# Moving the SBUF slots of a three-stage kernel's matmul operands to multiples of 512 bytes

## The chip, the cores and the metric

The kernel runs on one NeuronCore of a Trainium2 chip. The metric is the device time of one execution in microseconds (us). TensorE is PE in the profile, its weight loads are PEld, VectorE is DVE, ScalarE is ACT, GpSimd is POOL and SyncE, which issues nearly all transfers, is SP.

## The reference

Four sequences of 3072 tokens with 256 features pass through three stages.

```python
scores = (1.0 / S) * np.matmul(z, z.transpose(0, 2, 1))     # z: 4 x 3072 x 64
out = u * np.matmul(np.maximum(scores, 0.0) ** 2, v)        # u, v: 4 x 3072 x 256
h = out @ w_in                                              # 256 -> 2048
x = (h - np.tanh(h)) @ w_out                                # 2048 -> 256
xk = mu_k * x + (1.0 - mu_k) * x_prev                       # x_prev: the token before, 0 at a sequence's start
xr = mu_r * x + (1.0 - mu_r) * x_prev
k = np.maximum(xk @ w_k, 0.0)                               # 256 -> 1024
result = 1.0 / (1.0 + np.exp(-(xr @ w_r))) * (k * k @ w_v)  # 1024 -> 256
```

`u`, `v`, `z` and the mixing vectors are float32. The weights are float64, and the kernel makes float32 of their high and low words during the attention.

## The kernel before

The work is cut into 24 blocks of 512 tokens (six a sequence). Features, or keys, lie on the 128 partitions and tokens along a partition, so every matmul has a moving operand of 128x512 and a stationary one of 128x128, both float32 read in one pass. To keep precision each operand is split into a high and a low part, and a product takes three matmuls (`PASSES`: high by high, high by low, low by high); the scores put both parts of the 64 features of z on the 128 partitions and take two.

A unit is `produce`, which writes a two-bank PSUM tile `w` and makes from it a high part `h` and a low part `l` of 128x1024 (on ACT and DVE), and `consume`, 12 matmuls that add the unit's product into `acc`. Units are A (attention, two chunks of 128 keys, 4 matmuls at L323 and L324), H (the 256 to 2048 to 256 feed-forward, 12 matmuls at L334), K (the channel mix, 12 matmuls at L334) and R (the gate, 12 matmuls at L358, and no consume). The loop issues `produce` of unit n and then `consume` of unit n-2 (`LAG`), all of it at L390. There are 288 A units, then for each of the 24 blocks 8 H, 4 K and 1 R; the K and R of a block are woven into the H of the next. That is 288x16 + 24x300 = 11808 matmuls, and 4584 of them stand before the first H matmul (288 produces of 4, 286 consumes of 12). PE's order is written out by this loop. All other work hangs on steps with a first and a last unit, which `run_steps` hands out after each unit by their costs; the engines run their queues in order.

Memory is a row of slots in each partition, in the order in which the pools first ask for them, each rounded up to 32 bytes. `mu` and `omu` (16 bytes each) come first, and everything else stands behind them. A slot's start, as the remainder by 512:

| tiles | what they are for matmuls | remainder before |
|---|---|---|
| `v`, `w_in`, `w_out`, `w_k`, `w_v` (tag big) | stationary | 32 |
| `h`, `l` of all units (tags hi, lo) | moving, at L390 | 32 |
| `xh`, `x`, `mkh`, `mkl`, `mrh`, `mrl` (tag p4) | moving, at L334 and L358 | 192 |
| `z1`, `z2` (tag p2, 11 slots) | both, at L323 and L324 | 192, 224, 256, ... 480, 0: 32 more from slot to slot |
| `w_r` (tag p2) | stationary, at L358 | 320 (high), 384 (low) |

The p2 slots walk because the tag also holds `x2`, which has 4 columns more than 512: 2064 bytes. Within a tile every operand begins at a multiple of 512 bytes from the tile's start, so these remainders are those of the operands.

`x2_steps` copies a block's H result from PSUM to `x2` (L412) behind a column 3 that holds the token ahead of the block: DVE copies it from the block before (L414) or writes 0 (L416). `mix_steps` then makes the mixed tokens: ACT scales the shifted columns 3 to 514 by `omu` (L430), DVE adds `mu` times the unshifted ones (L433), and two more steps split the sum into high and low.

Of the kernel before, what the change touches and what calls it, by code (L numbers as in the profile page):

```python
# [7 lines left out]
F32 = mybir.dt.float32  # L8
# [3 lines left out]
ACTF = mybir.ActivationFunctionType  # L12
ALU = mybir.AluOpType

P = 128
TB = 512
# [3 lines left out]
def relu2_attention__tanh_ffn__channel_mix_kernel(  # L20
# [20 lines left out]
    nc = tc.nc  # L41
# [4 lines left out]
    DC = D // P  # L46
    NG = S // TB
# [4 lines left out]
    scale = 1.0 / S  # L52
# [5 lines left out]
    sb = ctx.enter_context(tc.tile_pool(name="sb", bufs=1))  # L58
# [6 lines left out]
    def p4(name, dt=F32, shape=(P, 2, 512)):  # L65
        return sb.tile(list(shape), dt, tag="p4", name=name, bufs=10)

    def p2(name, dt=F32, n=512):
        return sb.tile([P, n], dt, tag="p2", name=name, bufs=NG + 5)

    mu = sb.tile([P, 2, DC], F32, name="mu")
    omu = sb.tile([P, 2, DC], F32, name="omu")
    x1d = [dr.tile([P, DC, TB], F32, name=f"x1d{t}") for t in range(NT)]

    def copy_hi(o, i):
# [2 lines left out]
    def sub_lo(o, i, hi):  # L78
        nc.vector.tensor_tensor(out=o, in0=i, in1=hi.bitcast(F32), op=ALU.subtract)  # L79
# [4 lines left out]
    def z_load(b, g):  # L84

        t = sb.tile([P, 16, 32], F32, tag="zs", name=f"zin{b}_{g}", bufs=3)
        src = z[b, g * TB : (g + 1) * TB, :].rearrange("(k j) (a i) -> a j k i", j=32, i=32)
        for h in range(P // DQ):
            for a in range(DQ // 32):
                q = nc.scalar if h and b == 0 and g == 0 else nc.sync  # L90
                q.dma_start(out=t[h * DQ + 32 * a : h * DQ + 32 * a + 32], in_=src[a])  # L91
        zin[b, g] = t

    def z_steps(b, g):
        st = {}

        def high():
            a = zin.pop((b, g))
            st["t"] = t = sb.tile([P, TB], F32, tag="zt", name=f"zt{b}_{g}", bufs=1)
            st["w"] = w = p2(f"z1_{b}_{g}", F32R)  # L100
            nc.vector.transpose(out=t, in_=a.rearrange("p k i -> p (k i)"))
            nc.vector.tensor_copy(w, t)

        def low():
            t, w = st["t"], st["w"]
            sub_lo(w[DQ:], t[DQ:], w[DQ:])
            if b == 0 and g == 0:
                z2[0] = w2 = p2("z2_0", F32R)
                sub_lo(w2[:DQ], t[:DQ], w[:DQ])
                copy_hi(w2[DQ:], t[DQ:])  # L110
            z1[b, g] = w

        return [(1.0, high), (0.7, low)]
# [8 lines left out]
    def v_load(b, g):  # L122
        t = p4(f"vr{b}_{g}", shape=(P, 4, D))
        nc.sync.dma_start(
            out=t, in_=v[b, g * TB : (g + 1) * TB, :].rearrange("(c p) d -> p c d", p=P)
        )
        vraw[b, g] = t

    def v_steps(b, g):
        st = {}  # L130

        def high():
            st["w"] = w = big(f"v{b}_{g}").rearrange("p (l c d) -> p l c d", l=2, c=4)
            copy_hi(w[:, 0], vraw[b, g])

        def low():
            w = st["w"]
            sub_lo(w[:, 1], vraw.pop((b, g)), w[:, 0])
            vs[b, g] = w

        return [(0.0, high), (1.3, low)]
# [127 lines left out]
    xraw, xs, x2t, mixed = {}, {}, {}, {}  # L269
# [105 lines left out]
    def consume(unit):  # L375
        kind, t, p = unit
        if kind == "R":
            return
        s = split.pop(unit)
        o = get_acc(kind, t)  # L380
        last = {"A": NP, "H": NH, "K": NK}[kind] - 1
        for j in range(2):
            f = 2 * p + j
            if kind == "A":
                w = [vs[t // NG, f // 4][:, l, f % 4] for l in range(2)]
            else:
                w = [x[:, f % 4] for x in ws["out" if kind == "H" else "v", f // 4]]
            for c in range(DC):
                for n, (a, m) in enumerate(PASSES):
                    nc.tensor.matmul(  # L390
                        o[:, c],
                        w[a][:, c * P : (c + 1) * P],
                        s[m][:, j],
                        start=p == 0 and j == 0 and n == 0,
                        stop=p == last and j == 1 and n == 2,
                    )
# [9 lines left out]
    def x2_steps(i):  # L406
        def f():
            o = acc.pop(("H", i))
            x2t[i] = []
            for c in range(DC):  # L410
                x = p2(f"x2_{i}_{c}", n=TB + 4)
                nc.scalar.activation(out=x[:, 4:], in_=o[:, c], func=ACTF.Copy)  # L412
                if i % NG:
                    nc.vector.tensor_copy(x[:, 3:4], x2t[i - 1][c][:, TB + 3 :])  # L414
                else:
                    nc.vector.memset(x[:, 3:4], 0.0)  # L416
                x2t[i].append(x)

        return [(0.2, f)]

    def mix_steps(which, i):
        m = 0 if which == "k" else 1
        st = {}

        def one(c):
            x = x2t[i][c]
            if c == 0:
                st["t"] = p4(f"mx{which}{i}")
            t = st["t"]
            nc.scalar.activation(  # L430
                out=t[:, c], in_=x[:, 3 : TB + 3], func=ACTF.Copy, scale=omu[:, m, c : c + 1]
            )
            nc.vector.scalar_tensor_tensor(  # L433
                out=t[:, c], in0=x[:, 4:], scalar=mu[:, m, c : c + 1], in1=t[:, c],
                op0=ALU.mult, op1=ALU.add,
            )

        def high():
            st["h"] = p4(f"m{which}h{i}", F32R)
            nc.vector.tensor_copy(st["h"], st["t"])  # L440

        def low():
            h, l = st["h"], p4(f"m{which}l{i}", F32R)
            sub_lo(l, st["t"], h)
            mixed[which, i] = (h, l)

        return [(0.8, lambda: one(0)), (0.8, lambda: one(1)), (0.8, high), (1.3, low)]
# [73 lines left out]
    for b in range(1, B):  # L521
        prev = (b - 1) * NG * NP
        last = prev + (NG - 1) * NP
        for g in range(NG):
            n = last - 3 * NP // 2 + 3 * g if g < 3 else last + 2 * (g - 3) + 2
            load(n - 3, z_load, b, g)
            task(n, b * NG * NP + 2 * g - 1 if g else b * NG * NP - 5, z_steps, b, g)
            n = prev + NP + ((NG - 2) * NP * g) // NG
# [20 lines left out]
    for i in range(NT):  # L549
        n = at["H", i, 0]  # L550
        load(n - 8, x_load, i)
        task(n - 5, n - 1, x_steps, i)
        n = at["H", i, NH - 1] + LAG
# [3 lines left out]
        n = at["K", i, NK - 1] + LAG  # L557
# [4 lines left out]
    def run_steps(n):  # L562

        for x in [x for x in tasks if x[1] <= n]:
            tasks.remove(x)
            ready.append((x[0], list(x[3](*x[4]))))
        ready.sort(key=lambda x: x[0])
        kind = units[min(n, len(units) - 1)][0]
        left = {"A": 1.4, "H": 2.2, "K": 2.4, "R": 4.0}[kind]
        while ready and (left > 0 or ready[0][0] <= n):  # L570
            for x in list(ready):
                if left > 0 or x[0] <= n:
                    cost, f = x[1].pop(0)
                    f()
                    left -= cost
                    if not x[1]:
                        ready.remove(x)

    with tc.manual_schedule():
        z_load(0, 0)  # L580
        z_load(0, 1)
        v_load(0, 0)
        z_load(0, 2)
        v_load(0, 1)
        for cost, f in z_steps(0, 0) + z_steps(0, 1) + v_steps(0, 0):
            f()
        for m, src in ((0, moe2_mu_k), (1, moe2_mu_r)):
            with nc.allow_non_contiguous_dma(reason="a column of the mixing vector"):
                nc.sync.dma_start(out=mu[:, m, :], in_=src.rearrange("(c p) -> p c", p=P))
        for n in range(len(units) + LAG + 3):  # L590
            for f in loads.pop(n, ()):
                f()
            if n < len(units):
                produce(units[n])
            if LAG <= n < len(units) + LAG:
                consume(units[n - LAG])
            if n == 1:
                nc.vector.tensor_scalar(
                    out=omu, in0=mu, scalar1=-1.0, scalar2=1.0, op0=ALU.mult, op1=ALU.add
                )  # L600
            run_steps(n)
        assert not loads and not tasks and not ready
# [29 lines left out]
```

## Time and profile before

| | us |
|---|---|
| median of 3 runs (2741.99 to 2742.69) | 2742.02 |
| profiled execution, own time | 2742.86 |
| its span, first to last instruction | 2741.1 |
| PE busy in the span | 2725.4 |
| DVE busy | 1694.7 |
| ACT busy | 1363.3 |

The own time is 1.76 us above the span: what lies before the first and behind the last instruction. Busy times of engines overlap. A matmul's duration in the rows (0.39 us and more) runs from its start to the end of its pipeline and overlaps the next one, so the pace of PE is read from the starts. In a timeline, a row with x2 holds two instructions that run into each other.

### The profile page before, as it was taken

Reading aid. Unit: us, or ns where it says so; the run is one execution under the profiler, and the core shown is the slowest. Engines: PE = TensorE matmul, PEld = TensorE weight load, DVE = VectorE, ACT = ScalarE, POOL = GpSimd, SP = SyncE. Lnnn points to the kernel's source line nnn. Section 1 sums busy time; section 2 is a strip of 40 time slices with the busy share of each in tenths; the row PEclk is TensorE's granted clock in tenths of the full one; section 3 lists DMA queues with packets and bytes.
Section 4 is the critical chain, followed back from the end, with each engine's and each line's share of the span. In section 5 each row is a group of like instructions: output and inputs, shape, how many; then the busy total and the mean of one; then the engine's idle time right before and its main releaser. Section 6 shows DMA issues by size and latency. Waiting matters only on the chain.

```text
span 2741.1 us, 29086 instructions
## 1 busy us (share of the span) xinstructions
PE 2725.4 (99%) x11808; PEld 2220.4 (81%) x11808; DVE 1694.7 (62%) x1923; ACT 1363.3 (50%) x1386; POOL 0.2 (0%) x4
## 2 busy tenths in 40 slices
PE   8999999999999999999999999999999999999998
PEld 7888888888888888888888888888888888888887
DVE  8788778877876556555555555555555555555554
ACT  6555556556556555444444444444444444444443
POOL 0000000000000000000000000000000000000000
PEclk9999999999999999999999999999999999999999
DMA  6242233332241101000000000000000000000001
GB/s 119 67 103 54 71 84 81 70 81 70 69 96 44 43 12 77 8 16 16 16 16 16 16 16 16 16 16 16 16 16 16 16 16 16 16 16 16 16 8 16
DMA packets 288118, 103.35 MB, mean 38 GB/s; under 512 B 256880, under 2 KB 269168, under 8 KB 287984
## 3 DMA queue, kind: packets, MB, share of 16 engines
q1 hardware_dynamic: 286928, 101.36, 16.3%
q8 instruction: 92, 1.51, 0.2%
q14 instruction: 42, 0.34, 0.0%
q10 hardware_dynamic: 1056, 0.13, 0.0%
HBM read 63.70 MB, written 31.72 MB: 35 GB/s over the span
## 4 chain that ended last, share of the span: by engine, by line
PE 99%; DMA 0%; SPq 0%; DVE 0%; ACT 0%; issue 0%; DVEq 0%
PE acc_A L390 29%; PE w_H L334 20%; PE acc_H L390 19%; PE w_K L334 10%; PE acc_K L390 10%; PE w_A L323 5%; PE w_A L324 5%; PE w_R L358 2%; DMA vr<-in_v_dram 0%; SPq L91 0%; DVE ot L466 0%; DVE o L456 0%; ACT v L76 0%; ACT r_A L308 0%; ACT a_A L309 0%
## 5 line engine op out<-in xcount | busy, mean ns | idle before, releaser
L390 PE MATMUL acc_A<-h_A,v 128*128 128x512 f32 x2304 | 762.5, 392 | 0.0
L334 PE MATMUL w_H<-xh,w_in 128*128 128x512 f32 x1536 | 511.2, 396 | 0.0
L390 PEld LDWEIGHTS acc_A<-h_A,v 128*128 128x128 f32 x2304 | 432.9, 188 | 96.5
L390 PE MATMUL acc_H<-h_H,w_out 128*128 128x512 f32 x1536 | 505.5, 390 | 0.0
L308 ACT ACTIVATE r_A<-w_A 128x1024 f32<-128x1024 f32 (+1 forms) x289 | 296.3, 1025 | 411.6 <-PE w_A L324 411.6
L390 PE MATMUL acc_A<-l_A,v 128*128 128x512 f32 x1152 | 450.7, 391 | 0.0
L76 ACT ACTIVATE h_H<-g_H 128x1024 fp32r<-128x1024 f32 x192 | 203.6, 1060 | 371.7 <-DVE g_H L348 371.7
L79 DVE TENSOR_TENSOR l_H<-g_H,h_H 128x1024 fp32r<-128x1024 f32 x192 | 235.3, 1226 | 216.3 <-ACT h_H L76 216.3
L79 DVE TENSOR_TENSOR l_A<-a_A,h_A 128x1024 fp32r<-128x1024 f32 (+1 forms) x289 | 353.1, 1222 | 9.9
L310 DVE CAST h_A<-a_A 128x1024 fp32r<-128x1024 f32 (+1 forms) x289 | 199.5, 690 | 235.5 <-ACT a_A L309 234.8
L348 DVE TENSOR_TENSOR g_H<-w_H,g_H 128x1024 f32<-128x1024 f32 x192 | 233.6, 1216 | 180.0 <-ACT g_H L347 179.9
L334 PEld LDWEIGHTS w_H<-xh,w_in 128*128 128x128 f32 x1536 | 288.6, 188 | 68.2
L390 PEld LDWEIGHTS acc_H<-h_H,w_out 128*128 128x128 f32 x1536 | 288.4, 188 | 63.3
L347 ACT ACTIVATE g_H<-w_H 128x1024 f32<-128x1024 f32 x192 | 195.9, 1020 | 269.8 <-PE w_H L334 269.8
L309 ACT ACTIVATE a_A<-r_A 128x1024 f32<-128x1024 f32 (+1 forms) x289 | 305.9, 1058 | 9.2
L334 PE MATMUL w_H<-x,w_in 128*128 128x512 f32 x768 | 304.3, 396 | 0.0
L390 PE MATMUL acc_H<-l_H,w_out 128*128 128x512 f32 x768 | 300.0, 391 | 0.0
L334 PE MATMUL w_K<-mkh,w_k 128*128 128x512 f32 x768 | 257.2, 396 | 0.0
L390 PEld LDWEIGHTS acc_A<-l_A,v 128*128 128x128 f32 x1152 | 216.5, 188 | 48.8
L390 PE MATMUL acc_K<-h_K,w_v 128*128 128x512 f32 x768 | 252.8, 390 | 0.0
L324 PE MATMUL w_A<-z,z 128*128 128x512 f32 x576 | 228.3, 396 | 0.0
L310 DVE CAST h_K<-a_K 128x1024 fp32r<-128x1024 f32 x96 | 66.7, 695 | 250.6 <-ACT a_K L309 250.6
(111 smaller groups left out, 2680.6 us busy)
## 6 DMA issues: line engine op xcount, KB each, us to landing
vr<-in_v_dram SPq DMA_DIRECT2D x24, 512.0 KB, 5.3
uin<-in_u_dram SPq DMA_DIRECT2D x192, 64.0 KB, 3.3
x1d<-x SPq DMA_DIRECT2D x24, 512.0 KB, 2.9
x<-x1d SPq DMA_DIRECT2D x24, 512.0 KB, 3.8
out_dram<-ot SPq DMA_DIRECT2D x192, 64.0 KB, 2.0
zin<-in_z_dram SPq DMA_DIRECT2D x94, 64.0 KB, 3.0
z<-z SPq DMA_DIRECT2D x46, 128.0 KB, 5.6
c_in<-in_moe_w_in_dram SPq DMA_DIRECT2D x8, 512.0 KB, 5.2
```

The source lines that it names most:

```text
L76: nc.scalar.activation(out=o, in_=i, func=ACTF.Copy)
L79: nc.vector.tensor_tensor(out=o, in0=i, in1=hi.bitcast(F32), op=ALU.subtract)
L308: nc.scalar.activation(out=r[:, x], in_=w[:, x], func=ACTF.Relu, scale=sc)
L309: nc.scalar.activation(out=a[:, x], in_=r[:, x], func=ACTF.Square)
L310: nc.vector.tensor_copy(h[:, x], a[:, x])
L323: nc.tensor.matmul(w[:, j], lhsT, z1[b, g], start=True, stop=False)
L324: nc.tensor.matmul(w[:, j], lhsT, z2[t], start=False, stop=True)
L334: nc.tensor.matmul(w[:, j], ws[wt, f // 4][a][:, c, (f % 4) * P : (f % 4 + 1) * P], x[m][:, c], start=n == 0, stop=n == 3 * DC - 1,)
L347: nc.scalar.activation(out=g, in_=w, func=ACTF.Tanh)
L348: nc.vector.tensor_tensor(out=g, in0=w, in1=g, op=ALU.subtract)
L358: nc.tensor.matmul(w[:, d], ws["r", 0][a][:, c, d * P : (d + 1) * P], x[m][:, c], start=n == 0, stop=n == 3 * DC - 1,)
L390: nc.tensor.matmul(o[:, c], w[a][:, c * P : (c + 1) * P], s[m][:, j], start=p == 0 and j == 0 and n == 0, stop=p == last and j == 1 and n ...
```

## The change

`mu`, `omu` and a column `zero` become parts of one tile `head` of 96 float32, 384 bytes; behind it the next slot begins at a multiple of 512. `x2` loses its four extra columns, so a p2 slot has 2048 bytes. With that every tile of the table above has remainder 0, in every slot. The token ahead is no longer copied: the scaling on ACT is done in two instructions, one for columns 1 to 511 of the block (511 columns) and one for column 0, which reads the last column of the block before, or `zero`.

```diff
-    mu = sb.tile([P, 2, DC], F32, name="mu")
-    omu = sb.tile([P, 2, DC], F32, name="omu")
+    head = sb.tile([P, 96], F32, name="head")
+    mu = head[:, : 2 * DC].rearrange("p (m c) -> p m c", m=2)
+    omu = head[:, 2 * DC : 4 * DC].rearrange("p (m c) -> p m c", m=2)
+    zero = head[:, 4 * DC : 4 * DC + 1]
...
-                x = p2(f"x2_{i}_{c}", n=TB + 4)
-                nc.scalar.activation(out=x[:, 4:], in_=o[:, c], func=ACTF.Copy)
-                if i % NG:
-                    nc.vector.tensor_copy(x[:, 3:4], x2t[i - 1][c][:, TB + 3 :])
-                else:
-                    nc.vector.memset(x[:, 3:4], 0.0)
+                x = p2(f"x2_{i}_{c}")
+                nc.scalar.activation(out=x, in_=o[:, c], func=ACTF.Copy)
...
-            nc.scalar.activation(
-                out=t[:, c], in_=x[:, 3 : TB + 3], func=ACTF.Copy, scale=omu[:, m, c : c + 1]
-            )
+            w = omu[:, m, c : c + 1]
+            ahead = x2t[i - 1][c][:, TB - 1 :] if i % NG else zero
+            nc.scalar.activation(out=t[:, c, 1:], in_=x[:, : TB - 1], func=ACTF.Copy, scale=w)
+            nc.scalar.activation(out=t[:, c, :1], in_=ahead, func=ACTF.Copy, scale=w)
             nc.vector.scalar_tensor_tensor(
-                out=t[:, c], in0=x[:, 4:], scalar=mu[:, m, c : c + 1], in1=t[:, c],
+                out=t[:, c], in0=x, scalar=mu[:, m, c : c + 1], in1=t[:, c],
                 op0=ALU.mult, op1=ALU.add,
             )
...
             if n == 1:
+                nc.vector.memset(zero, 0.0)
```

PE and SP have the same instructions in the same order in both kernels. On ACT, where block 1 is mixed (names carry the block and a buffer number; `mxk` and `mxr` are the mixed tokens of K and R), before:

```order
L412 ACTIVATE x2_1_0_9208<-acc_H1_8860 128x512
L412 ACTIVATE x2_1_1_9211<-acc_H1_8860 128x512
L430 ACTIVATE mxk1_9214<-x2_1_0_9208,omu_64 128x512
L430 ACTIVATE mxr1_9217<-x2_1_0_9208,omu_64 128x512
L430 ACTIVATE mxk1_9214<-x2_1_1_9211,omu_64 128x512
L430 ACTIVATE mxr1_9217<-x2_1_1_9211,omu_64 128x512
```

and with the change:

```order
L416 ACTIVATE x2_1_0_9210<-acc_H1_8861 128x512
L416 ACTIVATE x2_1_1_9212<-acc_H1_8861 128x512
L432 ACTIVATE mxk1_9214<-x2_1_0_9210,head_63 128x511
L433 ACTIVATE mxk1_9214<-x2_0_0_8826,head_63 128x1
L432 ACTIVATE mxr1_9218<-x2_1_0_9210,head_63 128x511
L433 ACTIVATE mxr1_9218<-x2_0_0_8826,head_63 128x1
L432 ACTIVATE mxk1_9214<-x2_1_1_9212,head_63 128x511
L433 ACTIVATE mxk1_9214<-x2_0_1_8828,head_63 128x1
L432 ACTIVATE mxr1_9218<-x2_1_1_9212,head_63 128x511
L433 ACTIVATE mxr1_9218<-x2_0_1_8828,head_63 128x1
```

Each of the four scalings has a second instruction of one column behind it, which reads block 0's tile (`x2_0_0`, `x2_0_1`). On DVE, at the same block, before:

```order
L79 TENSOR_TENSOR l_K0_3_9164<-a_K0_3_9162,h_K0_3_9163 128x1024
L414 COPY x2_1_0_9208<-x2_0_0_8826 128x1
L414 COPY x2_1_1_9211<-x2_0_1_8829 128x1
L433 SCALAR_TENSOR_TENSOR mxk1_9214<-x2_1_0_9208,mu_63,mxk1_9214 128x512
L433 SCALAR_TENSOR_TENSOR mxr1_9217<-x2_1_0_9208,mu_63,mxr1_9217 128x512
L433 SCALAR_TENSOR_TENSOR mxk1_9214<-x2_1_1_9211,mu_63,mxk1_9214 128x512
L433 SCALAR_TENSOR_TENSOR mxr1_9217<-x2_1_1_9211,mu_63,mxr1_9217 128x512
```

and with the change:

```order
L83 TENSOR_TENSOR l_K0_3_9166<-a_K0_3_9164,h_K0_3_9165 128x1024
L434 SCALAR_TENSOR_TENSOR mxk1_9214<-x2_1_0_9210,head_63,mxk1_9214 128x512
L434 SCALAR_TENSOR_TENSOR mxr1_9218<-x2_1_0_9210,head_63,mxr1_9218 128x512
L434 SCALAR_TENSOR_TENSOR mxk1_9214<-x2_1_1_9212,head_63,mxk1_9214 128x512
L434 SCALAR_TENSOR_TENSOR mxr1_9218<-x2_1_1_9212,head_63,mxr1_9218 128x512
```

The two one-column copies ahead of the sums are gone; the sums and what follows them stand as they did.

## Rows read from the trace of the kernel before

**Rows 1.** The page: span, busy time of each engine, and the chain that ended last.

```profile
span 2741.1 us, 29086 instructions
...
PE 2725.4 (99%) x11808; PEld 2220.4 (81%) x11808; DVE 1694.7 (62%) x1923; ACT 1363.3 (50%) x1386; POOL 0.2 (0%) x4
...
PE 99%; DMA 0%; SPq 0%; DVE 0%; ACT 0%; issue 0%; DVEq 0%
...
```

**Rows 2.** The waits of PE, all of them: what, for what, us, times, longest.

```profile
...
PE w_A L323 <- DVE z L79: 6.5, 1, 6.5
PE w_A L323 <- ACT r_A L308: 1.0, 1, 1.0
```

**Rows 3.** Timeline of PE at the start: start us, us, instruction.

```profile
...
8.31 0.63 PE L324 MATMUL w_A<-z,z 128*128 128x512 f32 x1
...
9.16 0.63 PE L324 MATMUL w_A<-z,z 128*128 128x512 f32 x1
...
15.27 0.40 PE L390 MATMUL acc_A<-l_A,v 128*128 128x512 f32 x1
...
```

**Rows 4.** Timeline of PE, one unit of the first feed-forward block late in the run.

```profile
...
2300.70 0.40 PE L390 MATMUL acc_H<-h_H,w_out 128*128 128x512 f32 x1
...
2301.16 0.62 PE L390 MATMUL acc_H<-h_H,w_out 128*128 128x512 f32 x2
...
2303.20 0.39 PE L390 MATMUL acc_H<-h_H,w_out 128*128 128x512 f32 x1
2303.43 0.40 PE L334 MATMUL w_H<-xh,w_in 128*128 128x512 f32 x1
...
2306.23 0.39 PE L390 MATMUL acc_H<-h_H,w_out 128*128 128x512 f32 x1
...
```

**Rows 5.** Timeline of PE, two units of the attention.

```profile
...
99.22 0.61 PE L390 MATMUL acc_A<-h_A,v 128*128 128x512 f32 x2
...
101.26 0.39 PE L390 MATMUL acc_A<-h_A,v 128*128 128x512 f32 x1
...
102.41 0.39 PE L390 MATMUL acc_A<-h_A,v 128*128 128x512 f32 x1
...
105.17 0.39 PE L323 MATMUL w_A<-z,z 128*128 128x512 f32 x1
```

**Rows 6.** Timeline of PE: the first feed-forward matmul, and the last matmul of all.

```profile
...
1064.84 0.40 PE L334 MATMUL w_H<-xh,w_in 128*128 128x512 f32 x1
...
2732.62 0.39 PE L390 MATMUL acc_K<-h_K,w_v 128*128 128x512 f32 x1
```

**Rows 7.** Timeline of PE, the gate matmuls of the last token block.

```profile
...
2724.61 0.39 PE L358 MATMUL w_R<-mrh,w_r 128*128 128x512 f32 x1
...
2727.39 0.39 PE L390 MATMUL acc_K<-h_K,w_v 128*128 128x512 f32 x1
...
```

**Rows 8.** Groups by line and shape, ACT and DVE, whole span.

```profile
...
L308 ACT ACTIVATE r_A<-w_A 128x1024 f32<-128x1024 f32 x287 | 295.1, 1028 | 411.6 <-PE w_A L324 411.6
...
L430 ACT ACTIVATE mxk<-x,omu 128x512 f32<-128x512 f32 x48 | 34.6, 721 | 0.8 <-DVE x L414 0.4 <-DVE x L416 0.4
...
L414 DVE COPY x<-x 128x1 f32<-128x1 f32 x40 | 4.2, 145 | 0.0
...
L308 ACT ACTIVATE r_A<-w_A 128x512 f32<-128x512 f32 x2 | 1.2, 580 | 0.0
...
```

**Rows 9.** Timeline of ACT, two mixing instructions of one token block.

```profile
...
2359.98 0.72 ACT L430 ACTIVATE mxk<-x,omu 128x512 f32<-128x512 f32 x1
2360.60 0.72 ACT L430 ACTIVATE mxr<-x,omu 128x512 f32<-128x512 f32 x1
...
```

**Rows 10.** Timeline of DVE, a low part of the same block.

```profile
...
2377.98 1.23 DVE L79 TENSOR_TENSOR l_H<-g_H,h_H 128x1024 fp32r<-128x1024 f32 x1 [1.13 <-ACT h_H L76]
...
```

**Rows 11.** Timeline of PE, the matmul that reads that low part.

```profile
...
2381.28 0.40 PE L390 MATMUL acc_H<-l_H,w_out 128*128 128x512 f32 x1
...
```

**Rows 12.** One stretch of the attention: us, busy PE, PEld, DVE, ACT, POOL; clock, DMA, GB/s.

```profile
...
100.00:200.00 100.00, 100.00 (x438) 81.76 (x437) 83.25 (x106) 60.13 (x58) 0.00 (x0) 1.00 0.38 91
...
```

## The prediction

> **What bounds the kernel.** I read the page first: PE is busy for 2725.4 of 2741.1 us, and the chain that ended last is 99% PE [rows 1]. The waits say the same from the other side. PE waited twice, 6.5 us for the first z and 1.0 us for the first score squares, and never again [rows 2]. So the time is a start of 15 us, 11808 matmuls at some pace, and a tail; only the pace can give or cost more than a little. The next view is therefore the timeline of PE alone, and in it the distance from start to start.
>
> That distance is not one number, though all these matmuls have the same shape. The first ones, at the start, stand 0.425 us apart (two in 8.31 to 9.16 [rows 3]). [...] Late in the run, from 2301.16 to 2303.20, nine L390 starts take 2.04 us: 0.2267 each [rows 4]. The twelve L334 starts that follow take 2.80 us: 0.2333 [rows 4]. The L358 matmuls take 2.78 for twelve: 0.2317 [rows 7]. In the attention L390 again has a stretch of nine in 2.04 (99.22 to 101.26), yet in the next unit its twelve take 2.76, 0.230 each [rows 5]. No wait stands between any of them.
>
> Now lay the slot table beside it. At L390 the moving and the stationary operand both have remainder 32. At L334 they have 192 and 32, at L358 192 and 320 or 384, at L323 and L324 a different pair in every unit. Where both remainders agree, the pace settles at 0.2267 after some matmuls and stays until a product with other remainders comes; where they differ it does not settle. The three slower L390 starts at the head of the unit in [rows 4] (2300.70 to 2301.16 holds two of 0.23) are what is left over from the L334 before. [...]
>
> **The change, part by part.**
>
> *Remainders.* With the change all pairs agree. I take the settled pace of 0.2267 for every matmul after the slow start. The rows' hundredths leave 2.04 ± 0.01 over nine; two such stretches agree, so I give the pace ± 0.0004.
> First stretch, the attention: start 17 (by the code's order) is at 15.27 [rows 3], matmul 4585, the first of H, at 1064.84 [rows 6]. That is 4568 starts in 1049.6 us, 0.2298 each. At 0.2267 they take 1035.4: 14.2 us less.
> Second stretch: from 1064.84 to the last matmul at 2732.62 [rows 6], 7223 starts in 1667.8 us, 0.2309 each. At 0.2267 they take 1637.2: 30.6 us less.
> The sum is -44.8. The pace's ± 0.0004 over 11791 starts is ± 5.
>
> *The start and the tail* stay: the 16 slow matmuls follow the z and v loads, and from the last matmul to the end are 8.5 us of sums, transposes and stores that the change does not touch.
>
> *The added ACT work.* Each token block gets four one-column scalings. No row has that shape. From 128x1024 at 1028 ns and 128x512 at 580 ns [rows 8] a column costs 0.875 ns and what is left is 132 ns; a shape of one column is nearest to that rest, and I take 0.2 us for it, between 0 and the 0.58 of 512 columns. What covers it: the four scalings follow each other 0.62 us apart [rows 9], DVE's sums wait for them, the next g, h and l of an H unit stand in line behind those, and so PE could wait for an l. The tightest l I found ends at 2377.98 + 1.23 = 2379.21 [rows 10], and PE reads it at 2381.28 [rows 11]: 2.07 us of room. The faster PE takes 48 x 0.0042 = 0.2 of it and four small scalings 0.8. About 1.1 is left, so I cost it at nothing. At 0.58 each they would take 2.3, overdraw by 0.4 and cost 24 x 0.4 = 10 us.
>
> *The removed DVE work*, two copies of 145 ns a block [rows 8], gives a little of this back, and the scaling no longer waits for them (0.4 us once [rows 8]). Not on the path: 0. The last column of a block's `x2` is now read one block later, which holds two p2 slots longer, four of eleven where w_r has two: no wait.
>
> *DVE under a faster PE.* In the attention DVE is busy 83.25 of 100 us [rows 12]. With PE 1.4% faster it would be 84.4: still behind PE, cost 0.
>
> Against the profiled execution's own 2742.86 this is 2698.1; the median of the runs lies 0.84 below that one, so 2742.02 - 44.8 = 2697.2, and I predict 2697.
>
> [...]
>
> **The rivals.**
>
> *Nothing happens.* The paces would then belong to the lines (how a unit's three matmuls share their operands, a change of PSUM bank), not to the addresses: 2742, give or take 3. For it: L390 against L334 is also a difference of line. Against it: L390 alone runs at 0.2267 in one unit and 0.230 in the next [rows 5]; what differs there is the z pair in front of it.
>
> [...]
>
> *Only part settles.* If the attention settles but the products with p4 tiles do not, -14: 2728; the other way round, -31: 2711.
>
> [...]
>
> **How the numbers follow.** All pairs settle at 0.2267: 0.58, 2697, with 2691 to 2703 from its own pace, or to 2707 with the dear scalings. Part: 0.10. Nothing: 0.12. Slower: 0.13. More: 0.07. Faster by over 0.2% (5.5 us, about what a measurement of this kernel can tell from no change) is 0.58 + 0.10 + 0.07 = 0.75, the same 0.12, slower 0.13. The range leaves out slower and more, which is 0.20, and holds the rest: 2688 to 2748.
>
> **What the profile after would show.** Right: start-to-start distances of 0.2267 at the lines that L334 and L358 become as at the one that L390 becomes, from about 20 us to the end; a token block of 300 matmuls every 68.0 us where now it is 300 x 0.2309 = 69.3; the first H matmul at about 1050.6; still two waits of PE. Wrong in its main step: a long run at 0.23 or above with all remainders 0, at any line. Wrong in its cover: a wait of PE for an l of H, once a token block, behind scalings of one column that last much over 0.2 us.

## The result and the profile after

The changed kernel takes 2698.0 us (median of 4 runs, 2697.03 to 2698.34) against 2742.01 before: a ratio of 0.9838, 95% interval [0.9821, 0.9855], 44 us less. The forecast was 2697.

The page of the kernel after (span; busy times; the chain that ended last, by engine):

```profile
span 2696.2 us, 29132 instructions
...
PE 2681.1 (99%) x11808; PEld 2219.3 (82%) x11808; DVE 1698.1 (63%) x1876; ACT 1381.0 (51%) x1482; POOL 0.2 (0%) x4
...
PE 99%; DMA 0%; SPq 0%; DVE 0%; ACT 0%; issue 0%; DVEq 0%
...
```

It answers to [rows 1]: the span is 44.9 us shorter, PE's busy time 44.3, and the chain is 99% PE as it was. DVE and ACT did not become shorter (1694.7 and 1363.3 before), so nothing of the gain is theirs. The waits of PE (for what, us in total, times, longest) answer to [rows 2]:

```profile
...
PE w_A L327 <- DVE z L83: 6.0, 1, 6.0
PE w_A L327 <- ACT r_A L312: 1.1, 1, 1.1
```

Still the two waits of the start and no other. So the gain is pace: the distance from one matmul start to the next. The timeline of PE in a unit of H late in the run (start us, us, instruction; the first matmul of the twelve first products, of the twelve of the consume, and of what follows) answers to [rows 4]:

```profile
...
2062.41 0.39 PE L338 MATMUL w_H<-xh,w_in 128*128 128x512 f32 x1
...
2065.14 0.39 PE L394 MATMUL acc_H<-h_H,w_out 128*128 128x512 f32 x1
...
2067.86 0.39 PE L338 MATMUL w_H<-xh,w_in 128*128 128x512 f32 x1
```

L338 is the line that L334 became, and L394 the old L390. Twelve starts of the first and twelve of the second take 2.73 and 2.72 us, 0.2271 at the hundredths shown and the same for both, where they took 2.80 and 2.73 before. The long stretch gives the pace more closely, by the first matmul of H and the last of all, against [rows 6]:

```profile
...
1050.58 0.39 PE L338 MATMUL w_H<-xh,w_in 128*128 128x512 f32 x1
...
2687.79 0.39 PE L394 MATMUL acc_K<-h_K,w_v 128*128 128x512 f32 x1
```

7223 starts in 1637.21 us are 0.22667 each, to the last digit the pace of the settled stretches in [rows 4, 5]. At the start (against [rows 3]) the slow pace is what it was, 0.425:

```profile
...
7.83 0.63 PE L328 MATMUL w_A<-z,z 128*128 128x512 f32 x1
...
8.68 0.63 PE L328 MATMUL w_A<-z,z 128*128 128x512 f32 x1
...
14.81 0.63 PE L394 MATMUL acc_A<-l_A,v 128*128 128x512 f32 x1
15.24 0.77 PE L394 MATMUL acc_A<-h_A,v 128*128 128x512 f32 x2
...
```

Matmul 17 of the code's order stands here at 14.81 (the row of 15.24 holds matmuls 18 and 19); 15.27 before. That the first z came 0.5 us earlier is scatter of the loads: PE's first wait is 6.5, 6.0 and 6.8 us in the kernel before, this one and the run with the old places below.

What the change added, and its room. The timeline of ACT where a block is mixed, and the groups of the two scalings (count, busy us and mean ns) answer to [rows 8, 9]:

```profile
...
2321.99 0.72 ACT L432 ACTIVATE mxk<-x,head 128x511 f32<-128x511 f32 x1
2322.60 0.29 ACT L433 ACTIVATE mxk<-head 128x1 f32<-128x1 f32 x1
2322.79 0.71 ACT L432 ACTIVATE mxr<-x,head 128x511 f32<-128x511 f32 x1
...
```

```profile
...
L432 ACT ACTIVATE mxk<-x,head 128x511 f32<-128x511 f32 x48 | 34.4, 717 | 0.0
...
L433 ACT ACTIVATE mxk<-x,head 128x1 f32<-128x1 f32 x40 | 11.4, 285 | 0.0
...
```

A scaling of one column lasts 285 ns, but the next instruction starts 0.19 us after it, so four of them put 0.76 us into the line. The tightest low part I found, by the timelines of DVE and of PE, against [rows 10, 11]:

```profile
...
2340.57 1.23 DVE L83 TENSOR_TENSOR l_H<-g_H,h_H 128x1024 fp32r<-128x1024 f32 x1 [1.13 <-ACT h_H L80]
...
```

```profile
...
2342.80 0.39 PE L394 MATMUL acc_H<-l_H,w_out 128*128 128x512 f32 x1
...
```

It ends at 2341.80, and PE reads it at 2342.80: 1.00 us of room where there were 2.07.

### The profile page after: what moved, and what is told of

Read it like the earlier page. It is cut to its first block, busy times and chain, and to the rows that moved or that the text cites. A ratio compares the mean times of both kernels' runs of the same rounds, so it can differ in the third digit from the quotient of the medians.

```text
span 2696.2 us, 29132 instructions
## 1 busy us (share of the span) xinstructions
PE 2681.1 (99%) x11808; PEld 2219.3 (82%) x11808; DVE 1698.1 (63%) x1876; ACT 1381.0 (51%) x1482; POOL 0.2 (0%) x4
## 4 chain that ended last, share of the span: by engine, by line
PE 99%; DMA 0%; SPq 0%; DVE 0%; ACT 0%; issue 0%; DVEq 0%
PE acc_A L394 29%; PE acc_H L394 19%; PE w_H L338 19%; PE acc_K L394 10%; PE w_K L338 10%; PE w_A L327 5%; PE w_A L328 5%; PE w_R L362 2%; DMA vr<-in_v_dram 0%; SPq L95 0%; DVE ot L467 0%; DVE o L457 0%; ACT v L80 0%; ACT r_A L312 0%; ACT a_A L313 0%
## 5 line engine op out<-in xcount | busy, mean ns | idle before, releaser
L394 PE MATMUL acc_A<-h_A,v 128*128 128x512 f32 x2304 | 756.8, 389 | 0.0
L394 PEld LDWEIGHTS acc_A<-h_A,v 128*128 128x128 f32 x2304 | 433.3, 188 | 89.7
L394 PE MATMUL acc_H<-h_H,w_out 128*128 128x512 f32 x1536 | 504.0, 389 | 0.0
L338 PE MATMUL w_H<-xh,w_in 128*128 128x512 f32 x1536 | 500.4, 389 | 0.0
L394 PE MATMUL acc_A<-l_A,v 128*128 128x512 f32 x1152 | 448.6, 389 | 0.0
L394 PEld LDWEIGHTS acc_H<-h_H,w_out 128*128 128x128 f32 x1536 | 288.4, 188 | 59.7
L338 PEld LDWEIGHTS w_H<-xh,w_in 128*128 128x128 f32 x1536 | 288.4, 188 | 59.7
L338 PE MATMUL w_H<-x,w_in 128*128 128x512 f32 x768 | 298.8, 389 | 0.0
L394 PE MATMUL acc_H<-l_H,w_out 128*128 128x512 f32 x768 | 298.8, 389 | 0.0
L394 PEld LDWEIGHTS acc_A<-l_A,v 128*128 128x128 f32 x1152 | 216.9, 188 | 45.2
L394 PE MATMUL acc_K<-h_K,w_v 128*128 128x512 f32 x768 | 251.8, 389 | 0.0
L338 PE MATMUL w_K<-mkh,w_k 128*128 128x512 f32 x768 | 251.8, 389 | 0.0
```

The source lines that it names most:

```text
L338: nc.tensor.matmul(w[:, j], ws[wt, f // 4][a][:, c, (f % 4) * P : (f % 4 + 1) * P], x[m][:, c], start=n == 0, stop=n == 3 * DC - 1,)
L394: nc.tensor.matmul(o[:, c], w[a][:, c * P : (c + 1) * P], s[m][:, j], start=p == 0 and j == 0 and n == 0, stop=p == last and j == 1 and n ...
```

## The experiments

The theory: what sets the pace is the distance between two places, where a matmul's moving operand is read and where the next matmul's stationary one is (the two reads; the trace has them at the same time, 81.76 us of PEld in 100.00 of PE [rows 12]); where both have the same remainder PE settles at 0.2267. The rivals: each operand's own place at a multiple counts; or the new mixing made the gain; or another distance is better still. The times of the first four runs are medians of four, ten, two and two executions, beside 2742.39 of the kernel before. The other six are single executions, beside 2741.89 and 2741.63; executions of one kernel lie up to 2 us apart here, so of single times only larger differences are read.

**All operands at remainder 224.**

```diff
-    head = sb.tile([P, 96], F32, name="head")
+    head = sb.tile([P, 24], F32, name="head")
```

> The changed kernel with a head of 96 bytes, so that every operand begins at remainder 224 by 512: all pairs agree, none is at a multiple of 512 or even of 64. Theory (what counts is that the moving and the stationary operand have the same remainder): 2698 us, all starts 0.2267 apart. Rival (a start at a multiple counts, each operand by itself): the pace of before or worse, 2742 to 2775.

Measured: 2697.34, ratio to before 0.9836 [0.9822, 0.9851]. The timeline of PE, the same unit:

```profile
...
2061.71 0.39 PE L338 MATMUL w_H<-xh,w_in 128*128 128x512 f32 x1
...
2064.43 0.39 PE L394 MATMUL acc_H<-h_H,w_out 128*128 128x512 f32 x1
...
2067.15 0.39 PE L338 MATMUL w_H<-xh,w_in 128*128 128x512 f32 x1
```

2.72 and 2.72. No matmul operand begins at a multiple of 64 here, and the time is that of the change, 2698.0. A multiple is not needed; agreement at another place does the same.

**The new mixing with the old places.**

```diff
-    head = sb.tile([P, 96], F32, name="head")
+    head = sb.tile([P, 16], F32, name="head")
...
-        return sb.tile([P, n], dt, tag="p2", name=name, bufs=NG + 5)
+        return sb.tile([P, TB + 8], dt, tag="p2", name=name, bufs=NG + 5)[:, :n]
```

> The changed kernel, with its new mixing, but every slot where it was before: head of 64 bytes, p2 slots of 2080. Theory: the time of before, 2742, with 0.2333 at the first products of H and K and 0.2267 late in each unit of consume. Rival (the other order on DVE and ACT gave the time): 2698.

Measured: 2742.07, ratio 0.9999 [0.9989, 1.0008]. The timeline of PE:

```profile
...
2095.81 0.40 PE L338 MATMUL w_H<-xh,w_in 128*128 128x512 f32 x1
...
2098.62 0.39 PE L394 MATMUL acc_H<-h_H,w_out 128*128 128x512 f32 x1
...
2101.35 0.40 PE L338 MATMUL w_H<-xh,w_in 128*128 128x512 f32 x1
```

The first products are back at 2.81, the consume at 2.73, as in [rows 4]. Copies against one-column scalings is worth nothing that can be measured; the places give all of it.

**Half of the memory moved, by 256 and by 128.** A pad ahead of the big slots moves the weights, v, h and l against z, x and the mixed tokens, so the consumes still agree and the first products of H and K do not.

```diff
+    pads = []
+
     def big(name):
+        if not pads:
+            pads.append(sb.tile([P, 256 // 4], F32, tag="pad", name="pad", bufs=1))
```

> The changed kernel with 256 bytes of padding ahead of the big slots: weights and v, h and l at remainder 256, z, x and the mixed tokens at 0. If remainders have to agree by 256: 2698, 0.2267 everywhere. If by 512: the 3456 first products of H and K fall to about 0.2333 and the three starts behind each unit to 0.231, 23 + 4 us more, 2725.

> As the run before with 128 bytes of padding: big, h and l at 128, the rest at 0. If remainders have to agree by 256 (or 512): 0.23 and more at the first products of H and K, some 2715 to 2730. If agreeing by 128 or 64 is enough: 2698.

Measured: 2697.03 with 256 (ratio 0.9834 [0.9815, 0.9854]) and 2728.43 with 128 (0.9949 [0.9929, 0.9969]). The timelines of PE, 256 and then 128:

```profile
...
2061.44 0.39 PE L342 MATMUL w_H<-xh,w_in 128*128 128x512 f32 x1
...
2064.16 0.39 PE L398 MATMUL acc_H<-h_H,w_out 128*128 128x512 f32 x1
...
2066.88 0.39 PE L342 MATMUL w_H<-xh,w_in 128*128 128x512 f32 x1
```

```profile
...
2082.65 0.40 PE L342 MATMUL w_H<-xh,w_in 128*128 128x512 f32 x1
...
2083.11 0.63 PE L342 MATMUL w_H<-xh,w_in 128*128 128x512 f32 x2
...
2085.44 0.39 PE L398 MATMUL acc_H<-h_H,w_out 128*128 128x512 f32 x1
...
2088.18 0.40 PE L342 MATMUL w_H<-xh,w_in 128*128 128x512 f32 x1
```

With 256 the pace is that of the change. With 128 the first products take 2.79 for twelve, 0.2325, and the consume that follows 2.74. From the third of the twelve on, at 2083.11, ten starts take 2.33, 0.233 each. So remainders have to agree by 256 bytes here; by 128 or 64 is not enough, and by 512, as the change does it, is more than is needed.

**A constant distance everywhere but in the scores and the gate.** The big slots alone are moved, by 32, 64, 192 or 224, and a second pad behind them brings h and l back to 0. The distance is the stationary operand's start less the moving one's, by 256. z, w_r and the mixed tokens stay at 0, so the pairs within the scores and within the gate (1440 of the 11808 matmuls) still agree. The cut is that of 64.

```diff
+            pads.append(sb.tile([P, 64 // 4], F32, tag="pad", name="pad", bufs=1))
...
     def square_split(name, w, sc, pieces=1):
+        if len(pads) < 2:
+            pads.append(sb.tile([P, 448 // 4], F32, tag="pad2", name="pad2", bufs=1))
```

> The changed kernel with 32 bytes of padding ahead of the big slots and 480 behind them: weights and v at remainder 32, all moving operands (and z) at 0. A constant distance of 32 between the two reads, apart from the scores. Theory (only agreement settles at 0.2267): 0.230 or more, 2710 to 2750. Rival (some other distance keeps the two reads apart better): below 0.2267 at the first products and the consumes, below 2697, down to 2560.

> The same with 64 and 448: weights and v at 64. Theory: 0.230 or more, 2710 to 2750. Rival: below 0.2267, 2560 to 2697; single starts of 0.2258 after a start of this distance in the kernel before speak for it.

> The same with 192 and 320: weights and v at 192, which is 64 the other way round by 256. Theory: 0.230 or more, 2710 to 2750. Rival: below 0.2267, 2560 to 2697. If order matters, another time than at 64.

> The same with 224 and 288: weights and v at 224, 32 the other way round. Theory: 0.230 or more, 2710 to 2750. Rival: below 0.2267, 2560 to 2697. If order matters, another time than at 32.

Measured: 2768.78, 2770.64, 2720.34 and 2767.19. The timelines of PE in the same unit, in this order:

```profile
...
2115.51 0.40 PE L344 MATMUL w_H<-xh,w_in 128*128 128x512 f32 x1
...
2118.31 0.40 PE L400 MATMUL acc_H<-h_H,w_out 128*128 128x512 f32 x1
...
2121.11 0.40 PE L344 MATMUL w_H<-xh,w_in 128*128 128x512 f32 x1
```

```profile
...
2117.18 0.40 PE L344 MATMUL w_H<-xh,w_in 128*128 128x512 f32 x1
...
2117.65 0.63 PE L344 MATMUL w_H<-xh,w_in 128*128 128x512 f32 x2
2118.12 0.40 PE L344 MATMUL w_H<-x,w_in 128*128 128x512 f32 x1
...
2119.99 0.40 PE L400 MATMUL acc_H<-h_H,w_out 128*128 128x512 f32 x1
...
2122.78 0.40 PE L344 MATMUL w_H<-xh,w_in 128*128 128x512 f32 x1
```

```profile
...
2078.93 0.39 PE L344 MATMUL w_H<-xh,w_in 128*128 128x512 f32 x1
...
2081.67 0.39 PE L400 MATMUL acc_H<-h_H,w_out 128*128 128x512 f32 x1
...
2084.42 0.39 PE L344 MATMUL w_H<-xh,w_in 128*128 128x512 f32 x1
```

```profile
...
2114.05 0.39 PE L344 MATMUL w_H<-xh,w_in 128*128 128x512 f32 x1
...
2116.85 0.39 PE L400 MATMUL acc_H<-h_H,w_out 128*128 128x512 f32 x1
...
2119.65 0.39 PE L344 MATMUL w_H<-xh,w_in 128*128 128x512 f32 x1
```

24 starts take 5.60, 5.60, 5.49 and 5.60 us: 0.2333, 0.2333, 0.2288 and 0.2333. No mean is below 0.2267, so no distance tried here is better than 0. Three of four times lie above the 2750 that I had given them: I had taken the mixed distances of the kernel before as the bad case, but its consumes agree, and a kernel in which only the scores and the gate agree is slower than it, by 25 to 29 us. The direction counts as well: the stationary operand 64 behind (192) costs 22 us against the change, 64 ahead costs 73.

These runs settle two questions more. One is whether the work of DVE and ACT shows in the pace. They are busy for 63% and 51% of the change's time, and yet in its trace each of the 7223 starts after that of the first H matmul lies 0.226 or 0.227 us behind the one before; at 64, any two starts that the rows of the unit above keep apart take 0.46 or 0.47 (2117.18, 2117.65, 2118.12). What DVE and ACT happen to do leaves no mark in these starts. The other is whether a matmul's own weights count or the next one's: it is seen where one kind of matmul follows another, here in the attention of the run at 224:

```profile
...
502.51 0.39 PE L400 MATMUL acc_A<-h_A,v 128*128 128x512 f32 x1
...
502.96 0.39 PE L334 MATMUL w_A<-z,z 128*128 128x512 f32 x1
...
503.42 0.40 PE L334 MATMUL w_A<-z,z 128*128 128x512 f32 x1
...
503.89 0.40 PE L400 MATMUL acc_A<-l_A,v 128*128 128x512 f32 x1
...
```

The two starts from 502.51 take 0.45 us. The first is the last matmul of a consume: its own weights stand 224 off, the next ones (z) agree. The two from 503.42 take 0.47. The first is the last matmul of the scores: its own pair agrees, the next weights (v) stand 224 off. If the own weights counted, both would hold one slow and one settled start. Hundredths show little of this, but the trace of the kernel before has it in thousandths. The last matmul of a consume, whose own pair agrees at 32, is followed by the next start after 0.235 in all 24 places where the gate comes next (`w_r`, 320), and after 0.226 or 0.227 in all 264 where first products of H or K do (weights at 32). So it is the next weights that count here.

**Agreement missed by 16 bytes**, in the consumes alone. (The head is 256 bytes, which puts everything else at 384, or 128 by 256.)

```diff
-    head = sb.tile([P, 96], F32, name="head")
+    head = sb.tile([P, 64], F32, name="head")
...
-        h = sb.tile([P, 2, 512], F32R, tag="hi", name=f"h_{name}", bufs=3)
-        l = sb.tile([P, 2, 512], F32R, tag="lo", name=f"l_{name}", bufs=3)
-        return h, l
+        h = sb.tile([P, 1088], F32R, tag="hi", name=f"h_{name}", bufs=3)
+        l = sb.tile([P, 1088], F32R, tag="lo", name=f"l_{name}", bufs=3)
+        return [x[:, 4:1028].rearrange("p (j t) -> p j t", j=2) for x in (h, l)]
```

> The changed kernel with h and l begun 16 bytes behind all other operands (by 256: 144, the rest 128). If agreement is needed to the byte: the consumes and what follows each stand above 0.2267, some 2705 to 2765 by what distances of 32 do. If memory is met in pieces of 32 bytes or more: 0.2267 everywhere, 2697.

Measured: 2744.99. The timeline of PE:

```profile
...
2099.86 0.39 PE L338 MATMUL w_H<-xh,w_in 128*128 128x512 f32 x1
...
2102.60 0.39 PE L394 MATMUL acc_H<-h_H,w_out 128*128 128x512 f32 x1
...
2105.38 0.39 PE L338 MATMUL w_H<-xh,w_in 128*128 128x512 f32 x1
```

The twelve of the consume take 2.78, 0.2317, and the twelve first products, which agree but come behind a consume that does not, 2.74. Sixteen bytes are enough to lose the whole gain of the change (2744.99 beside 2741.63 of the kernel before).

**Half the stationary columns in the gate.** The gate matmuls load 64 columns in place of 128; every operand begins where it did.

```diff
                         nc.tensor.matmul(
-                            w[:, d],
-                            ws["r", 0][a][:, c, d * P : (d + 1) * P],
+                            w[: P // 2, d],
+                            ws["r", 0][a][:, c, d * P : d * P + P // 2],
...
-            nc.scalar.activation(out=s, in_=w, func=ACTF.Sigmoid)
+            nc.vector.memset(s[P // 2 :], 0.0)
+            nc.scalar.activation(out=s[: P // 2], in_=w[: P // 2], func=ACTF.Sigmoid)
```

> The changed kernel in which the 288 gate matmuls (L362) load 64 stationary columns in place of 128, with every start as before it; the gate of features 64 to 127 of each half is left out (zeros). [...] The whole time moves by 2 us at most: 2696 to 2698.

Measured: 2698.93. The timeline of PE from the first of the twelve gate matmuls of a block to the matmul behind them, and the groups of weight loads (count, busy us, mean ns):

```profile
...
2111.91 0.40 PE L362 MATMUL w_R<-mrh,w_r 128*64 128x512 f32 x1
...
2112.37 0.61 PE L362 MATMUL w_R<-mrh,w_r 128*64 128x512 f32 x2
2112.82 0.40 PE L362 MATMUL w_R<-mrl,w_r 128*64 128x512 f32 x1
2113.05 0.63 PE L362 MATMUL w_R<-mrh,w_r 128*64 128x512 f32 x2
2113.52 0.39 PE L362 MATMUL w_R<-mrl,w_r 128*64 128x512 f32 x1
...
2114.67 0.39 PE L395 MATMUL acc_H<-h_H,w_out 128*128 128x512 f32 x1
...
```

```profile
...
L395 PEld LDWEIGHTS acc_A<-h_A,v 128*128 128x128 f32 x2304 | 432.9, 188 | 90.5
...
L362 PEld LDWEIGHTS w_R<-mrh,w_r 128*64 128x64 f32 x192 | 25.7, 134 | 17.2
...
```

The load of 64 columns is shorter, 134 ns against 188, and the matmuls are farther apart: 2.76 for twelve, 0.230, where each start of the gate in the trace of the change is followed by the next after 0.226 or 0.227. They are not even either: two starts take 0.45 from 2112.37 and 0.47 from 2113.05, though the operands' starts agree here. So agreement was enough with loads of 128 columns and not with these; why is not shown. The whole time, 2698.93, lies above the 2696 to 2698 expected, but too near to the change's 2698.0 to tell; the 2 us in that expectation were my estimate, and no run shows what a weight column costs.

## Why the prediction was right

*The pace sets the time.* Right: the span fell by 44.9 us, and the starts account for 13.8 + 30.6 = 44.4 of it where 44.8 was forecast; the rest is the earlier first z, which is scatter. The attention's 4568 starts took 1035.8 us (14.81 to 1050.58) where 1035.4 was forecast, since one or two more of them were still slow (the first stood 0.43 from the next, 14.81 to 15.24), and the 7223 that follow took 1637.2 where 1637.2 was. A block of 300 matmuls now takes 300 x 0.22667 = 68.0.

*Where both remainders agree, the pace settles at 0.2267.* Right, and shown from both sides: agreement at another place has the same time (224), the old places with the new instructions have the time of before. The forecast took the remainder by 512; by 256 is enough. The size was right to the rows' last digit because the kernel before already ran at that pace in the second half of most consumes (in its trace the last six starts of 454 of its 576 consumes lie 0.226 or 0.227 apart), and the change spread it to all.

*Where they differ it does not settle.* Too short. At a constant distance PE holds a mean too, only a worse one: 0.2333 or 0.2288, with the twelve first products and the twelve of the consume of a unit alike to 0.02 us. The kernel before changed its distance with every twelve matmuls or fewer, and so it showed mostly the way from one to the other. This did not enter the sum.

*The rivals.* "Nothing happens" fell with the result: kernels that differ in padding alone run from 2697.03 to 2770.64 us. "Slower" (0.13), a time above that of before, did not come either: with all operands at 0 the kernel takes 2698.0 us and with all at 224 2697.34, so the place itself does not count in these runs. "Only part settles" was not what the change does. The pad of 128 comes near to that case, since the first products of H and K lose there, but that it took the 2728 of that rival is partly chance: the attention lost something too (the first H matmul stands at 1055.11 there, against 1050.58), and the first products ran at 0.2325 and not at the 0.2333 of before. "More" (0.07), a pace below 0.2267, found no support: no constant distance tried had a mean below 0.2267, and no run shows the lower pace that its chance, or the 2560 us of the rivals at 32 to 224, stands for.

*The added ACT work at nothing.* Right, with its terms: 0.2 us for a one-column scaling was 0.19 from start to start, and of 2.07 us of room 1.1 was forecast to be left and 1.00 was. The new mixing at the old places gives 0.9999 of the time.

*The cause behind it.* Not shown. The runs show what counts (the distance of the two starts by 256 bytes, to 16 bytes and with its sign) and not where in the chip the time is spent. The weight loads are not recorded as longer where the places differ: PEld is busy for 2220.4 us before and 2219.3 after. And with the half loads the gate runs at 0.230 though its starts agree, so agreement is not all of it.

## What to carry to other kernels

When PE never waits and its matmuls of one shape still start at different distances, look at where their operands begin: give a matmul's moving operand and the next matmul's stationary one the same remainder by 256 bytes, for all matmuls that follow each other (2698.0 us against 2742.01 here), and check it in the built layout, since one small tile asked for first or one slot that is 16 bytes too long moves everything behind it. A multiple is not needed (2697.34 with all at 224), agreement is. All of this was measured with float32 operands of the kernel's type F32R, moving operands of 128x512 and a load of 128x128 weights for each matmul; with loads of 64 columns agreement did not bring the settled pace (0.230 for 0.2267). To forecast what it brings, find a stretch of the old trace in which the operands agree by chance, and take the pace at its end for all.

## What the runs showed of the hardware that was not expected

A constant distance has a pace of its own: 0.2333 us between starts in the mean at 32, 64 and 224 bytes by 256, and 0.2288 at 192. So the direction counts: with the stationary operand 64 bytes ahead the pace is 0.2333, with it 64 behind 0.2288. Sixteen bytes in the consumes cost 47 us against the change (2744.99). And a weight load of half the columns, 54 ns shorter, came with matmuls that stand 0.003 us farther apart.
